# Weight conversion: the clamp on VectorE, the addition of the low words on GpSimd

## The chip, the cores and the metric

The kernel runs on one core of a Trainium2 chip. The time is the device time of one execution in microseconds (us); three executions of the kernel before took 1046.4, 1047.48 and 1050.78 us, and their median, 1047.48 us, is the time before. Engines are called by their names in the profile: PE is TensorE, DVE is VectorE, ACT is ScalarE, POOL is GpSimd, SP is SyncE, which here issues DMAs.

## The reference

Attention with mixing of heads on both sides of the softmax, and then a gated feed-forward block on its output. Cut to what is computed:

```python
scores = scale * np.matmul(q, k.transpose(0, 1, 3, 2))        # 4 batches, 12 heads, 448 x 448, head size 64
scores = np.einsum('bhij,hg->bgij', scores, w_pre)
attn   = softmax(scores)                                       # over the last axis
attn   = np.einsum('bhij,hg->bgij', attn, w_post)
x      = np.matmul(attn, v) -> 1792 tokens x 768
g      = x @ w_gate                                            # 768 x 1536
val    = x @ w_val                                             # 768 x 1536
out    = (silu(g) * val) @ w_out                               # 1536 x 768
```

The three feed-forward weights arrive as 64-bit floats (two 32-bit words each) and are made into 32-bit floats on the chip. This conversion is what the change touches.

## The kernel before

**Stages.** The attention of the four batches comes first, to about 510 us of the span. Then the tokens pass through the feed-forward block in two halves of 896 (`b` = 0 and 1). In each half the up part goes through 12 column blocks `f` of 128: per block four PE chains of 18 matmuls of 448 columns, two for the gate weight (`upg`, token halves 0 and 1) and two for the value weight (`upv`). One chain takes the high part of the weights (`whi`, L507), the low part (`wlo`, L508), and the high part with the low part of x (L512). ACT takes the silu of `upg` (`sg`, L517); DVE multiplies it with `upv` (`m`, L523), ACT rounds the product (`gh`, L528) and DVE takes the rest (`gl`, L534). The down part (`dn`, L546 to L548) follows.

**Units.** The weights are cut into 36 units of 128 x 768 numbers: units 0, 2, ... 22 are the gate weight of a block, 1, 3, ... 23 its value weight, 24 to 35 parts of `w_out`. So a block of the up part uses a pair of units, and a unit of `w_out` serves 63 matmuls. In the first half of the tokens each unit is loaded in its 64-bit form (`raw`) and converted by `convert` in nine steps; then it is stored to DRAM (`keep`) for the second half, which only loads it again. `split_w` makes `whi` on ACT (L492) and `wlo` on DVE (L488).

**The steps of `convert`.** Step 0 and 1 (ACT): absolute value (`mag`) and sign (`sgn`) of the word that holds the upper half. Step 2: clamp of `mag` from below and above (L460), one input, two operations. Steps 3 to 5 (DVE): bit shifts that make of `mag` the 32-bit float without its last bits, and in `w` its exponent (L462, L464, L466). Step 6 (DVE): the low word times the exponent (L468). Step 7 (DVE): `w = mag + w` (L470). Step 8: `w` times the sign (L472). Steps 2 and 8 are on `eng`: DVE for the units 0 to 2, which are converted beside the last batch's attention, POOL for the other 33. The tile `mag` has two buffers, `sgn` two, `w` three, `raw` two.

**Order.** Each piece of work is put on a list by `at(key, ...)` or `at_ff(key, ...)` with a number as its due time, and the list is worked off in the order of the numbers. So the numbers alone set in which order each engine gets its instructions; an engine then takes them one behind the other, and waits at each for what that one needs. `at_ff` counts the feed-forward block in matmul groups: a chain of the up part is 3.4 of them. For a unit that is due at `n`, a step with the number x is issued at `n - x`, the rounding to `whi` at `n - 3.8`, `wlo` at `n - 2.8`, the store at `n - 3.9`. All loads and stores of the weights go through SP's queue, in the order of the list.

Of the kernel before, what the change touches and what calls it, by code (L numbers as in the profile page):

```python
# [15 lines left out]
ALU = mybir.AluOpType  # L16
# [3 lines left out]
def f32_of(bits):  # L20
    return struct.unpack("<f", struct.pack("<I", bits))[0]
# [3 lines left out]
def talking_heads_moe_kernel(ctx, tc, q, k, v, w_pre, w_post, w_gate, w_val, w_out, out):  # L25
    nc = tc.nc
# [46 lines left out]
    def at(key, fn):  # L73
        ops.append((key, len(ops), fn))
# [7 lines left out]
    def later(fn, *a):  # L82
        return lambda: fn(*a)
# [267 lines left out]
    for b in range(B):  # L351
# [8 lines left out]
        for c in range(NC):  # L360

            n = n0 + first(c)
            if (b, c) == (0, 0):
                load, ready, step = -61, -31, 1.0
                score = -29.0
            else:
                before = tiles((c - 1) % NC)
                step = before / NPAIR
# [60 lines left out]
    def unit_index(u):  # L429
        if u[0] == "o":  # L430
            return 2 * NFC + u[1] * (NFC * ET // W) + u[2]
        return 2 * u[1] + (u[0] == "v")
# [9 lines left out]
    def convert(u, step):  # L442
        n = unit_index(u)
        eng = nc.vector if n < EARLY else nc.gpsimd
        if step == 0:
            mag, sgn, w = (
                pl["cv_p"].tile([P, W], F32, tag=x, name=f"{x}_{n}", bufs=k) for x, k in (("mag", 2), ("sgn", 2), ("w", 3))
            )
            cvs[u] = mag, sgn
            w32[0, u] = w  # L450
        mag, sgn = cvs[u]
        w = w32[0, u]
        low, high = raws[u][:, :, 0], raws[u].bitcast(F32)[:, :, 1]
        a, b = mag.bitcast(U32), w.bitcast(U32)
        if step == 0:
            nc.scalar.activation(mag, high, AF.Abs)  # L456
        elif step == 1:
            nc.scalar.activation(sgn, high, AF.Sign)
        elif step == 2:
            eng.tensor_scalar(mag, mag, f32_of(0x38000000), f32_of(0x47EFFFFF), op0=ALU.max, op1=ALU.min)  # L460
        elif step == 3:
            nc.vector.tensor_scalar(a, a, 0x08000000, 4, op0=ALU.bitwise_xor, op1=ALU.logical_shift_left)  # L462
        elif step == 4:
            nc.vector.tensor_scalar(b, a, 1, 0x7F800000, op0=ALU.logical_shift_right, op1=ALU.bitwise_and)  # L464
        elif step == 5:
            nc.vector.tensor_scalar(a, a, 1, None, op0=ALU.logical_shift_right)  # L466
        elif step == 6:
            nc.vector.scalar_tensor_tensor(w, low, 2.0 ** -52, w, op0=ALU.mult, op1=ALU.mult)  # L468
        elif step == 7:
            nc.vector.tensor_tensor(w, mag, w, op=ALU.add)  # L470
        else:
            eng.tensor_tensor(w, w, sgn, op=ALU.mult)  # L472

# [96 lines left out]
    def at_ff(n, fn):  # L570
        at(END + n / 1.8, fn)

    for b in range(NT // TB):
        n0 = b * span
        for i, (c, x) in enumerate((c, x) for c in range(NKC) for x in range(2)):
            if b:
                at_ff(n0 - 60 + 4.2 * i, later(load_x, b, x, c))
            else:
                at(B * NTB + (-2.8 + 0.9 * c if x else -9.6 + 1.2 * c), later(load_x, b, x, c))
        units = []  # L580
        for f in range(NFC):
            n = n0 + f * T_F
            units += [(n, ("g", f)), (n + 2 * T_H, ("v", f))]
            for hf in range(2):
                if b == f == hf == 0:
                    at(B * NTB + UPH, later(up, b, f, "g", hf, True, False))
                    at_ff(n, later(up, b, f, "g", hf, False, True))
                else:
                    at_ff(n + hf * T_H, later(up, b, f, "g", hf))
                at_ff(n + (2 + hf) * T_H, later(up, b, f, "v", hf))  # L590
                at_ff(n + (1 + hf) * T_H + 0.3, later(gate, b, f, hf))
                at_ff(n + (3 + hf) * T_H + 0.3, later(gated, b, f, hf))
                at_ff(n + (3 + hf) * T_H + 1.1, later(gated_low, b, f, hf))
        for e in range(3):
            n1 = n0 + NFC * T_F + e * NFC * T_D
            for f in range(0, NFC, W // ET):
                last = b == NT // TB - 1 and e == 2
                units.append((n1 + f * (0.6 if last else T_D), ("o", e, f // (W // ET))))
            if last:
                for c in range(NTC):  # L600
                    n = n1 + c * NFC * T_D / NTC
                    for f in range(NFC):
                        at_ff(n, later(down, b, e, f, c))
                    if c % 2 or c == NTC - 1:
                        at_ff(n + NFC * T_D / NTC + 0.1, later(finish, b, e, c - c % 2))
            else:
                for f in range(NFC):
                    for c in range(NTC):
                        at_ff(n1 + f * T_D, later(down, b, e, f, c))
                for c in range(0, NTC, 2):  # L610
                    at_ff(n1 + (NFC - 1 + (c + 2) / NTC) * T_D + 0.1, later(finish, b, e, c))
        for n, u in units:
            if b:
                at_ff(n - 16, later(load_w, b, u))
                at_ff(n - 8, later(split_w, b, u, False))
                at_ff(n - 7, later(split_w, b, u, True))
            elif unit_index(u) < EARLY:
                n = START + SPACE * unit_index(u)
                at(max(START, n - 4.0), later(load_raw, u))
                for step, x in enumerate((0.4, 0.8, 0.5, 0.5, 1.8, 2.5, 2.9, 4.1, 5.1)):  # L620
                    at(n + x + 0.25, later(convert, u, step))
                at(n + 8.4, later(split_w, b, u, False))
                at(n + 10.6, later(split_w, b, u, True))
                at(n + 6.7, later(keep, u))
            else:
                n -= LEAD
                n1 = END + (n - 21.3) / 1.8
                at(min(n1, B * NTB + 2.75) if unit_index(u) == EARLY else n1, later(load_raw, u))
                for step, x in enumerate((16.2, 15, 15.4, 12.6, 12.1, 11.6, 11.1, 10.2, 5.8)):
                    at_ff(n - x, later(convert, u, step))  # L630
                at_ff(n - 3.8, later(split_w, b, u, False))
                at_ff(n - 2.8, later(split_w, b, u, True))
                at_ff(n - 3.9, later(keep, u))
# [43 lines left out]
```

## Time and profile before

| | |
|---|---|
| time, median of three | 1047.48 us |
| the profiled execution | 1048.95 us, its span 1047.2 us |
| busy in the span | PE 97%, DVE 57%, ACT 49%, POOL 42% |
| last work of the attention on PE | at 510.6 us of the span |
| up part, first half of the tokens | to 686.7 us |
| down part, first half of the tokens | 686.7 to 776.3 us, then the second half |

The profile belongs to one execution. Its span is the time from the first to the last instruction; 1.75 us of the execution lie outside of it. A share of busy time is an average over all stages; what a change in one stage is worth is read from that stage. In the rows below, a row of a timeline has the start in us from the span's start, the duration in us, engine, line, operation, output<-inputs with their shapes, the number of instructions merged into the row, and in brackets how long the engine had been idle and what released it.

### The profile page before, as it was taken

To read this page: it belongs to the slowest core of one execution; us is meant where nothing else is said; L and a number is where in the kernel's file an instruction comes from. 1 tells how busy PE (TensorE), PEld (TensorE's weight loads), DVE (VectorE), ACT (ScalarE), POOL (GpSimd) and SP (SyncE) were. 2 spreads that over 40 slices of the span, in tenths; PEclk is the share of its full clock that TensorE was granted. 3 is DMA by queue.
4 is the path that set the end of the run, shared out by engine and by line. 5 is a ranking of instruction groups with operands and counts; after the bars stand their busy time and mean duration, and the time that the engine had idled before them with its cause. 6 is when DMAs were issued, how large, how long until landed. Compare 5 with 4: busy or idle time off the path is not lost.

```text
span 1047.2 us, 17964 instructions
## 1 busy us (share of the span) xinstructions
PE 1020.7 (97%) x6660; PEld 853.2 (81%) x6660; DVE 597.8 (57%) x1181; ACT 514.1 (49%) x1103; POOL 444.0 (42%) x439
## 2 busy tenths in 40 slices
PE   6899999999999999999999999999999999999998
PEld 3577777777777777777898888899999999999998
DVE  4566555657466565577499999998923322332110
ACT  2686776768676676786444434443322222222110
POOL 1675555647465555674375666667600000000000
PEclk9999999999999999998999999999999999999999
DMA  6466443844466443668554444448741112112311
GB/s 125 117 160 172 116 126 112 202 132 125 124 160 176 116 127 113 183 199 244 183 166 151 147 169 138 160 155 289 254 167 46 60 47 61 46 61 62 97 50 36
DMA packets 131055, 140.69 MB, mean 134 GB/s; under 512 B 52552, under 2 KB 114012, under 8 KB 130968
## 3 DMA queue, kind: packets, MB, share of 16 engines
q1 hardware_dynamic: 130776, 139.30, 45.3%
q8 instruction: 53, 0.87, 0.4%
q0 software_dynamic: 192, 0.24, 0.1%
q14 instruction: 34, 0.28, 0.1%
HBM read 70.19 MB, written 30.80 MB: 96 GB/s over the span
## 4 chain that ended last, share of the span: by engine, by line
PE 76%; DVE 13%; ACT 3%; issue 3%; DMA 3%; POOL 2%; SPq 0%; POOLq 0%; ACTq 0%; DVEq 0%
PE post L306 14%; PE qk L224 8%; PE av L328 7%; PE dn L547 5%; PE dn L546 5%; PE dn L548 5%; PE pre L271 5%; PE pre L273 3%; PE pre L272 3%; DVE w L470 3%; DVE mag L462 3%; PE upv L508 3%; PE upv L507 3%; PE upg L512 3%; PE upg L508 3%; PE upg L507 3%
## 5 line engine op out<-in xcount | busy, mean ns | idle before, releaser
L265 POOL TENSOR_TENSOR lo<-rs,hi 120x448 fp32r<-120x448 f32 x180 | 206.5, 1148 | 161.0 <-ACT hi L259 157.6
L306 PEld LDWEIGHTS post<-rw,e 120*112 120x112 f32 (+1 forms) x1440 | 169.9, 177 | 32.2 <-issue 9.6
L306 PE MATMUL post<-rw,e 120*112 120x120 f32 (+1 forms) x1440 | 181.7, 270 | 0.3 <-POOL rw L296 0.3
L460 POOL TENSOR_SCALAR mag<-mag 128x768 f32<-128x768 f32 x33 | 103.8, 3145 | 95.9 <-ACT mag L456 94.1
L547 PE MATMUL dn<-wlo,gh 128*128 128x256 f32 x504 | 141.1, 280 | 0.5 <-DVE wlo L488 0.5
L546 PE MATMUL dn<-whi,gh 128*128 128x256 f32 x504 | 141.0, 280 | 0.0
L548 PE MATMUL dn<-whi,gl 128*128 128x256 f32 x504 | 141.0, 280 | 0.0
L280 DVE TENSOR_REDUCE st<-pre 120x1 f32<-120x448 f32 x180 | 111.8, 621 | 39.8 <-PE pre L273 36.9
L315 ACT ACTIVATE attnT<-post 112x480 f32<-112x480 f32 (+3 forms) x192 | 103.5, 546 | 28.4 <-PE post L306 26.3
L287 ACT ACTIVATE e<-pre,st 120x448 f32<-120x448 f32 x180 | 114.0, 633 | 0.5 <-DVE st L280 0.5
L259 ACT ACTIVATE hi<-rs 120x448 fp32r<-120x448 f32 x180 | 103.9, 577 | 17.7 <-DMA rs<-stg 9.6
L508 PE MATMUL upv<-x,wlo 128*128 128x448 f32 x288 | 106.5, 370 | 4.7 <-DVE wlo L488 4.7
L488 DVE TENSOR_TENSOR wlo<-w,whi 128x768 fp32r<-128x768 f32 x72 | 69.1, 961 | 72.2 <-ACT whi L492 70.8
L230 DVE COPY stg<-qk 110x448 f32<-110x448 f32 (+1 forms) x144 | 85.1, 619 | 43.1 <-PE qk L224 42.5
L507 PE MATMUL upg<-x,whi 128*128 128x448 f32 x288 | 105.8, 367 | 0.0
L508 PE MATMUL upg<-x,wlo 128*128 128x448 f32 x288 | 105.6, 367 | 0.0
L507 PE MATMUL upv<-x,whi 128*128 128x448 f32 x288 | 105.6, 367 | 0.0
L224 PE MATMUL qk<-kk,qt 64*110 64x448 f32 (+1 forms) x384 | 100.3, 594 | 4.4 <-DVE stg L230 2.8
L492 ACT ACTIVATE whi<-w 128x768 fp32r<-128x768 f32 x72 | 60.2, 839 | 87.8 <-POOL w L472 57.9
L528 ACT ACTIVATE gh<-m 128x448 fp32r<-128x448 f32 x48 | 27.8, 579 | 137.8 <-DVE m L523 137.8
L547 PEld LDWEIGHTS dn<-wlo,gh 128*128 128x128 f32 x504 | 94.7, 188 | 0.7 <-DVE wlo L488 0.7
L546 PEld LDWEIGHTS dn<-whi,gh 128*128 128x128 f32 x504 | 94.7, 188 | 0.0
(65 smaller groups left out, 1786.7 us busy)
## 6 DMA issues: line engine op xcount, KB each, us to landing
rs<-stg SPq DMA_DIRECT2D x176, 210.0 KB
w_d<-w SPq DMA_DIRECT2D x36, 384.0 KB
w<-w_d SPq DMA_DIRECT2D x36, 384.0 KB
x<-x_d SPq DMA_DIRECT2D x24, 448.0 KB
x_d<-xs SPq DMA_DIRECT2D x42, 224.0 KB
raw<-in_moe_w_gate_dram SPq DMA_DIRECT2D x12, 768.0 KB
raw<-in_moe_w_val_dram SPq DMA_DIRECT2D x12, 768.0 KB
raw<-in_moe_w_out_dram SPq DMA_DIRECT2D x12, 768.0 KB
```

Of the source, the lines that this page charges most:

```text
L224: nc.tensor.matmul(pt[:m], qt[b, c][hs, p, :m], kk[b, p][hs], start=True, stop=True)
L259: nc.scalar.activation(hi[:n], x[:n], AF.Copy)
L265: nc.gpsimd.tensor_tensor(lo[:n], x[:n], hi[:n].bitcast(F32), op=ALU.subtract)
L280: nc.vector.tensor_reduce(st[:n, 0:1], pt[:n], axis=AX.X, op=ALU.max, negate=True)
L287: nc.scalar.activation(e[:n], pt[:n], AF.Exp, bias=st[:n, 0:1], scale=1.0, accum_out=st[:n, 1:2])
L306: nc.tensor.matmul(pt[:, c, :, :m], e[:n, c * CP:(c + 1) * CP], w[:n, :, :m], start=True, stop=True)
L460: eng.tensor_scalar(mag, mag, f32_of(0x38000000), f32_of(0x47EFFFFF), op0=ALU.max, op1=ALU.min)
L507: nc.tensor.matmul(pt, hi[:, c], xh[:, c, ts], start=(c == 0), stop=False)
L508: nc.tensor.matmul(pt, lo[:, c], xh[:, c, ts], start=False, stop=False)
L546: nc.tensor.matmul(pt, gh, hi, start=opens, stop=False)
L547: nc.tensor.matmul(pt, gh, lo, start=False, stop=False)
L548: nc.tensor.matmul(pt, gl, hi, start=False, stop=closes)
```

## The change

Two of the nine steps of `convert` change their engine for the units 3 to 35. The clamp (L460) goes from POOL to DVE, where it is issued together with the first bit shift; the addition (L470, now L469) goes from DVE to POOL. The units 0 to 2 keep both on DVE. The nine steps become eight, and the due numbers of the steps are set anew: the multiplication with the sign is now due at `n - 9.2` and no longer at `n - 5.8`. Lines behind the change have one number less than before (L488 becomes L487).

```diff
--- before.py
+++ after.py
@@ -457,17 +457,16 @@
         elif step == 1:
             nc.scalar.activation(sgn, high, AF.Sign)
         elif step == 2:
-            eng.tensor_scalar(mag, mag, f32_of(0x38000000), f32_of(0x47EFFFFF), op0=ALU.max, op1=ALU.min)
+            nc.vector.tensor_scalar(mag, mag, f32_of(0x38000000), f32_of(0x47EFFFFF), op0=ALU.max, op1=ALU.min)
+            nc.vector.tensor_scalar(a, a, 0x08000000, 4, op0=ALU.bitwise_xor, op1=ALU.logical_shift_left)
         elif step == 3:
-            nc.vector.tensor_scalar(a, a, 0x08000000, 4, op0=ALU.bitwise_xor, op1=ALU.logical_shift_left)
+            nc.vector.tensor_scalar(b, a, 1, 0x7F800000, op0=ALU.logical_shift_right, op1=ALU.bitwise_and)
         elif step == 4:
-            nc.vector.tensor_scalar(b, a, 1, 0x7F800000, op0=ALU.logical_shift_right, op1=ALU.bitwise_and)
+            nc.vector.tensor_scalar(a, a, 1, None, op0=ALU.logical_shift_right)
         elif step == 5:
-            nc.vector.tensor_scalar(a, a, 1, None, op0=ALU.logical_shift_right)
+            nc.vector.scalar_tensor_tensor(w, low, 2.0 ** -52, w, op0=ALU.mult, op1=ALU.mult)
         elif step == 6:
-            nc.vector.scalar_tensor_tensor(w, low, 2.0 ** -52, w, op0=ALU.mult, op1=ALU.mult)
-        elif step == 7:
-            nc.vector.tensor_tensor(w, mag, w, op=ALU.add)
+            eng.tensor_tensor(w, mag, w, op=ALU.add)
         else:
             eng.tensor_tensor(w, w, sgn, op=ALU.mult)
 
@@ -617,7 +616,7 @@
             elif unit_index(u) < EARLY:
                 n = START + SPACE * unit_index(u)
                 at(max(START, n - 4.0), later(load_raw, u))
-                for step, x in enumerate((0.4, 0.8, 0.5, 0.5, 1.8, 2.5, 2.9, 4.1, 5.1)):
+                for step, x in enumerate((0.4, 0.8, 0.7, 1.6, 2.3, 2.9, 4.1, 5.1)):
                     at(n + x + 0.25, later(convert, u, step))
                 at(n + 8.4, later(split_w, b, u, False))
                 at(n + 10.6, later(split_w, b, u, True))
@@ -626,7 +625,7 @@
                 n -= LEAD
                 n1 = END + (n - 21.3) / 1.8
                 at(min(n1, B * NTB + 2.75) if unit_index(u) == EARLY else n1, later(load_raw, u))
-                for step, x in enumerate((16.2, 15, 15.4, 12.6, 12.1, 11.6, 11.1, 10.2, 5.8)):
+                for step, x in enumerate((14.6, 14.2, 14.0, 13.4, 12.8, 12.2, 11.2, 9.2)):
                     at_ff(n - x, later(convert, u, step))
                 at_ff(n - 3.8, later(split_w, b, u, False))
                 at_ff(n - 2.8, later(split_w, b, u, True))
```

In the up part this is what stands on DVE for block 5 (its products `m_5_0` and `m_5_1`) and for the units 13 and 14, before (unit 13 is `mag_7045` and `w_7047`):

```order
L523 TENSOR_TENSOR m_5_0_7068<-sg_5_0_7007,upv_5_0_7013 128x448
L534 TENSOR_TENSOR gl_5_7071<-m_5_0_7068,gh_5_7070 128x448
L462 TENSOR_SCALAR mag_7045<-mag_7045 128x768
L523 TENSOR_TENSOR m_5_1_7099<-sg_5_1_7034,upv_5_1_7049 128x448
L464 TENSOR_SCALAR w_7047<-mag_7045 128x768
L534 TENSOR_TENSOR gl_5_7071<-m_5_1_7099,gh_5_7070 128x448
L466 TENSOR_SCALAR mag_7045<-mag_7045 128x768
L468 SCALAR_TENSOR_TENSOR w_7047<-raw_7011,w_7047 128x768
L470 TENSOR_TENSOR w_7047<-mag_7045,w_7047 128x768
L488 TENSOR_TENSOR wlo_13_7108<-w_6986,whi_13_7107 128x768
L462 TENSOR_SCALAR mag_7112<-mag_7112 128x768
L464 TENSOR_SCALAR w_7114<-mag_7112 128x768
```

and after (unit 13 is `mag_7071` and `w_7073`, unit 14 begins at `mag_7134`):

```order
L522 TENSOR_TENSOR m_5_0_7065<-sg_5_0_7004,upv_5_0_7017 128x448
L533 TENSOR_TENSOR gl_5_7068<-m_5_0_7065,gh_5_7067 128x448
L460 TENSOR_SCALAR mag_7071<-mag_7071 128x768
L461 TENSOR_SCALAR mag_7071<-mag_7071 128x768
L463 TENSOR_SCALAR w_7073<-mag_7071 128x768
L465 TENSOR_SCALAR mag_7071<-mag_7071 128x768
L522 TENSOR_TENSOR m_5_1_7101<-sg_5_1_7036,upv_5_1_7045 128x448
L467 SCALAR_TENSOR_TENSOR w_7073<-raw_7010,w_7073 128x768
L533 TENSOR_TENSOR gl_5_7068<-m_5_1_7101,gh_5_7067 128x448
L487 TENSOR_TENSOR wlo_13_7109<-w_7008,whi_13_7108 128x768
L460 TENSOR_SCALAR mag_7134<-mag_7134 128x768
L461 TENSOR_SCALAR mag_7134<-mag_7134 128x768
```

The clamp stands ahead of the first shift of each unit, the addition is gone, and the second product `m_5_1` and its rest now stand around the multiplication of the low words (L467), behind the three shifts and no longer between them. `wlo` of a unit stands, as before, behind the last DVE step of the next unit.

On POOL there stood in the same place, two operations to a unit, the clamp of one unit and the sign of the unit ahead of it (`w_6986` is unit 12, `w_7047` 13):

```order
L460 TENSOR_SCALAR mag_7045<-mag_7045 128x768
L472 TENSOR_TENSOR w_6986<-w_6986,sgn_6985 128x768
L460 TENSOR_SCALAR mag_7112<-mag_7112 128x768
L472 TENSOR_TENSOR w_7047<-w_7047,sgn_7046 128x768
L460 TENSOR_SCALAR mag_7173<-mag_7173 128x768
L472 TENSOR_TENSOR w_7114<-w_7114,sgn_7113 128x768
```

and now, again two to a unit, both of the same one (`w_7008` is unit 12, `w_7073` 13, `w_7136` 14):

```order
L469 TENSOR_TENSOR w_7008<-mag_7006,w_7008 128x768
L471 TENSOR_TENSOR w_7008<-w_7008,sgn_7007 128x768
L469 TENSOR_TENSOR w_7073<-mag_7071,w_7073 128x768
L471 TENSOR_TENSOR w_7073<-w_7073,sgn_7072 128x768
L469 TENSOR_TENSOR w_7136<-mag_7134,w_7136 128x768
L471 TENSOR_TENSOR w_7136<-w_7136,sgn_7135 128x768
```

At the end of the attention, DVE had before, with the first three operations of unit 3 (`mag_6350`) ahead of the fourth of the last attention outputs (`xs_3_3`):

```order
L340 TENSOR_TENSOR xs_3_1_6269<-av_3_1_6260,xs_3_1_6269 128x112
L340 TENSOR_TENSOR xs_3_2_6282<-av_3_2_6273,xs_3_2_6282 128x112
L462 TENSOR_SCALAR mag_6350<-mag_6350 128x768
L464 TENSOR_SCALAR w_6352<-mag_6350 128x768
L466 TENSOR_SCALAR mag_6350<-mag_6350 128x768
L340 TENSOR_TENSOR xs_3_3_6295<-av_3_3_6286,xs_3_3_6295 128x112
L468 SCALAR_TENSOR_TENSOR w_6352<-raw_6243,w_6352 128x768
```

and now:

```order
L340 TENSOR_TENSOR xs_3_1_6269<-av_3_1_6260,xs_3_1_6269 128x112
L340 TENSOR_TENSOR xs_3_2_6282<-av_3_2_6273,xs_3_2_6282 128x112
L340 TENSOR_TENSOR xs_3_3_6295<-av_3_3_6286,xs_3_3_6295 128x112
L460 TENSOR_SCALAR mag_6371<-mag_6371 128x768
L461 TENSOR_SCALAR mag_6371<-mag_6371 128x768
L463 TENSOR_SCALAR w_6373<-mag_6371 128x768
L465 TENSOR_SCALAR mag_6371<-mag_6371 128x768
L467 SCALAR_TENSOR_TENSOR w_6373<-raw_6243,w_6373 128x768
```

The fourth of these outputs stands ahead of unit 3 now. On ACT the absolute value of unit 3 has moved behind it in the same way.

## Rows read from the trace of the kernel before

**Rows 1.** The page's first part: busy us of each engine, share of the span, instructions.

```profile
PE 1020.7 (97%) x6660; PEld 853.2 (81%) x6660; DVE 597.8 (57%) x1181; ACT 514.1 (49%) x1103; POOL 444.0 (42%) x439
```

**Rows 2.** The timeline of PE in the middle of the up part: the last six matmuls of each chain, and the matmul that had to wait.

```profile
580.80 1.38 PE L512 MATMUL upg<-x,whi 128*128 128x448 f32 x6
...
584.45 1.38 PE L512 MATMUL upg<-x,whi 128*128 128x448 f32 x6
...
586.65 0.47 PE L508 MATMUL upv<-x,wlo 128*128 128x448 f32 x1 [0.62 <-DVE wlo L488]
...
588.99 1.18 PE L512 MATMUL upv<-x,whi 128*128 128x448 f32 x5
```

**Rows 3.** The same view at the second and at the last of the twelve blocks.

```profile
521.52 1.38 PE L512 MATMUL upg<-x,whi 128*128 128x448 f32 x6
...
673.62 1.38 PE L512 MATMUL upg<-x,whi 128*128 128x448 f32 x6
```

**Rows 4.** The timeline of DVE over one pair of units, from the first shift of a unit to the same shift two units on.

```profile
586.90 2.20 DVE L462 TENSOR_SCALAR mag<-mag 128x768 uint32<-128x768 uint32 x1 [0.30 <-POOL mag L460]
589.13 0.56 DVE L464 TENSOR_SCALAR w<-mag 128x768 uint32<-128x768 uint32 x1
589.73 0.56 DVE L466 TENSOR_SCALAR mag<-mag 128x768 uint32<-128x768 uint32 x1
590.20 0.95 DVE L468 SCALAR_TENSOR_TENSOR w<-raw,w 128x768 f32<-128x768 uint32 x1
591.19 1.46 DVE L470 TENSOR_TENSOR w<-mag,w 128x768 f32<-128x768 f32 x1
592.57 0.94 DVE L488 TENSOR_TENSOR wlo<-w,whi 128x768 fp32r<-128x768 f32 x1
593.44 0.61 DVE L523 TENSOR_TENSOR m<-sg,upv 128x448 f32<-128x448 f32 x1
594.70 1.40 DVE L534 TENSOR_TENSOR gl<-m,gh 128x448 fp32r<-128x448 f32 x1 [0.65 <-ACT gh L528]
596.01 0.55 DVE L462 TENSOR_SCALAR mag<-mag 128x768 uint32<-128x768 uint32 x1
596.48 0.61 DVE L523 TENSOR_TENSOR m<-sg,upv 128x448 f32<-128x448 f32 x1
597.01 0.55 DVE L464 TENSOR_SCALAR w<-mag 128x768 uint32<-128x768 uint32 x1
597.74 0.62 DVE L534 TENSOR_TENSOR gl<-m,gh 128x448 fp32r<-128x448 f32 x1 [0.18 <-ACT gh L528]
598.28 0.55 DVE L466 TENSOR_SCALAR mag<-mag 128x768 uint32<-128x768 uint32 x1
598.75 0.95 DVE L468 SCALAR_TENSOR_TENSOR w<-raw,w 128x768 f32<-128x768 uint32 x1
599.73 1.46 DVE L470 TENSOR_TENSOR w<-mag,w 128x768 f32<-128x768 f32 x1
...
602.36 2.20 DVE L462 TENSOR_SCALAR mag<-mag 128x768 uint32<-128x768 uint32 x1 [0.30 <-POOL mag L460]
```

**Rows 5.** The timeline of POOL over the same stretch.

```profile
583.88 2.98 POOL L460 TENSOR_SCALAR mag<-mag 128x768 f32<-128x768 f32 x1 [3.74 <-ACT mag L456]
586.83 1.85 POOL L472 TENSOR_TENSOR w<-w,sgn 128x768 f32<-128x768 f32 x1
590.45 3.33 POOL L460 TENSOR_SCALAR mag<-mag 128x768 f32<-128x768 f32 x1 [1.77 <-ACT mag L456]
593.76 1.85 POOL L472 TENSOR_TENSOR w<-w,sgn 128x768 f32<-128x768 f32 x1
```

**Rows 6.** Two rows of the timelines of POOL and DVE in the attention, where a subtraction on POOL and a `wlo` meet.

```profile
475.69 1.13 POOL L265 TENSOR_TENSOR lo<-rs,hi 120x448 fp32r<-120x448 f32 x1 [0.55 <-ACT hi L259]
476.04 1.60 DVE L488 TENSOR_TENSOR wlo<-w,whi 128x768 fp32r<-128x768 f32 x1
```

**Rows 7.** The instructions of the lines of the clamp and of the sign: duration in ns (least, median, most), first and last start.

```profile
L460 POOL TENSOR_SCALAR mag<-mag x33: 2776/3183/3346, 505.8 to 749.5; 128x768 f32<-128x768 f32 x33
L460 DVE TENSOR_SCALAR mag<-mag x3: 548/555/690, 450.7 to 474.4; 128x768 f32<-128x768 f32 x3
L472 POOL TENSOR_TENSOR w<-w,sgn x33: 1837/1848/2438, 516.1 to 759.3; 128x768 f32<-128x768 f32 x33
```

**Rows 8.** The timelines at the end of the attention: one row of PE, and three of DVE.

```profile
510.56 0.99 PE L328 MATMUL av<-attnT,vn 112*64 112x112 f32 x16 [1.39 <-DVE xs L340]
508.58 0.56 DVE L462 TENSOR_SCALAR mag<-mag 128x768 uint32<-128x768 uint32 x1 [2.44 <-POOL mag L460]
510.24 0.27 DVE L340 TENSOR_TENSOR xs<-av,xs 128x112 fp32r<-128x112 f32 x1
511.41 0.96 DVE L470 TENSOR_TENSOR w<-mag,w 128x768 f32<-128x768 f32 x1
```

**Rows 9.** Busy us of the engines in three stretches: length, PE, its weight loads, DVE, ACT, POOL, then the granted clock of PE as a share of full speed, share and GB/s of the DMA engines.

```profile
471.00:474.38 3.38, 1.69 (x12) 1.43 (x12) 3.35 (x6) 3.38 (x10) 3.38 (x4) 0.95 0.93 272
474.40:478.00 3.60, 3.60 (x21) 2.71 (x22) 3.53 (x8) 2.08 (x5) 1.88 (x3) 0.50 0.95 270
...
686.66:776.30 89.64, 89.14 (x758) 88.94 (x757) 68.29 (x72) 30.66 (x40) 50.49 (x20) 1.00 0.65 220
```

**Rows 10.** The waits of PE behind the first half's up part: who waited for whom, us in total, times, longest.

```profile
PE dn L547 <- DVE wlo L488: 0.5, 1, 0.5
```

## The prediction

> **What bounds the kernel now.** The page's first part is read first: PE is busy 97% of the span, every other engine under 60% [rows 1]. So a change off PE can only alter the little time in which PE waits, and the question is where it waits for the conversion. The waits of PE and then its timeline show that. In the up part of the first half a chain of 18 matmuls takes 3.65 us, start to start (580.80 to 584.45), but the first value chain of each block takes 4.54 (584.45 to 588.99), since its second matmul waits for `wlo` from DVE [rows 2]. Unhindered a block takes 4 x 3.65 = 14.60. From block 1 to block 11 the trace has 673.62 - 521.52 = 152.10 us for ten blocks, 6.10 more than 146.0 [rows 3]; with the 0.89 of the last block the conversion costs PE 7.0 us here. That is all that a faster conversion can win in this part.
>
> Next is the timeline of DVE over one pair of units, which is one block [rows 4]. From 586.90 to 602.36 it is 15.46 us, and DVE is hardly idle: 0.30 + 0.65 + 0.18 = 1.13. So a pair of units takes as long as DVE needs, and PE is held to that. But several rows are longer than the same instruction elsewhere: L462 takes 2.20 and 0.55, L534 1.40 and 0.62, L470 1.46 both times against 0.96 where POOL stands still [rows 4, 8]. The surplus is 1.65 + 0.78 + 2 x 0.50 = 3.43, and it falls together with POOL's operations [rows 5]. What is left, 15.46 - 1.13 - 3.43 = 10.90, is DVE's own work.
>
> **How the two engines exclude each other.** The multiplication L472 starts at 586.83 and takes 1.85; L462, issued at 586.90, ends at 589.10 and needs 0.55, so it was let in at 588.55, 1.72 behind POOL's start and 0.13 before its end. The next L472 starts at 593.76; L534, issued at 594.70, ends at 596.10 and needs 0.62, so again it got in at 595.48, 1.72 behind [rows 4, 5]. A subtraction on POOL, also with two inputs, let a `wlo` in 1.00 behind its start, again 0.13 before its end [rows 6]. So a POOL operation on two tiles keeps such DVE operations out nearly for its whole length. The clamp does not. The one at 590.45 is held up first: L468 runs to 591.15, and the clamp takes 3.33 instead of its least 2.78 [rows 4, 5, 7]; then L470, issued at 591.19, waits only to 591.69. So the clamp keeps DVE out for 0.54, and who asks first goes first. The product `m`, which reads PSUM, takes 0.61 beside POOL and without it [rows 4].
>
> **Term 1: the pair of units.** On DVE's own work: an addition goes; L468 to L488 takes 592.57 - 590.20 = 2.37, less the wait of 0.50 is 1.87, and 0.87 remains without the addition (L488 to the next row), so 2 x 1.00 is saved. A clamp comes, 0.55 by the three that DVE has done [rows 7], with the gap to the shift behind it 0.59, so 2 x 0.59 is added. The second `m` and `gl` now stand elsewhere; their neighbours overlap less or more by some 0.08 each, together +0.07. Own work: 10.90 - 2.00 + 1.18 + 0.07 = 10.15. Idle: the 0.65 for `gh` stays, the 0.30 for POOL's clamp goes, some 0.1 for `whi` stays: 0.75.
>
> The waits decide. The trace has no addition of these tiles on POOL. Its bounds are the shortest hold and the longest in the rows, 0.54 (the clamp) and 1.72 (L472); I take 1.72, since L472 has the same shape and two inputs and the subtraction behaved alike; less than 0.54 is excluded, as two tiles must be read. So POOL holds 4 x 1.72 = 6.88 per pair, against 2 x (1.72 + 0.54) = 4.52. Laid along the new order: (a) behind L467 of the pair's second unit comes `wlo`, issued before the addition; the addition waits for it and runs beside `m` and the idle time for `gh`; `gl` meets its last 0.37. (b) The multiplication follows behind `gl`; the clamp of the next unit, issued 0.08 before `gl` ends, waits for all of it, 1.64. (c) Behind that unit's L467 `gl` is first, then the addition, then `wlo`, which waits 1.56: it cannot come earlier, because its `whi` stands on ACT behind a `gh` that waits for `m`. (d) The multiplication follows on `wlo`, and the next clamp waits 1.64. Sum 5.21. A pair takes 10.15 + 0.75 + 5.21 = 16.1 us: DVE works less and waits more. PE then waits 1.5 in each block.
>
> Block 3 is the first to feel it (1.05), eight follow: 1.05 + 8 x 1.50 = 13.05. Against 7.0 this is **+6.05**. POOL, with 4 x 1.85 per pair, stays far from full; ACT's waits for the sign go, but nothing hung on them.
>
> The Trainium skill says otherwise of the clamp: by "SBUF — State Buffer", section "Who interferes with whom", a GpSimd operation and a VectorE operation of these kinds exclude each other for the whole instruction, whoever issues first. For the multiplication the trace agrees (1.72 of 1.85); for the clamp it does not, as L470 waited 0.50 at one that had over two us to run and `wlo` ran beside it in 0.94. By that rule the clamp would be the long hold, 2.78, and its removal a gain; this is the first rival's case.
>
> **Term 2: the end of the attention.** PE stood 1.39 because an output copy on DVE (510.24) was queued behind unit 3's L462, which waited 2.44 for POOL's clamp [rows 8]. This copy now stands ahead of unit 3: **-1.4**. Unit 3 itself is needed a block later. Bounds -1.4 and 0.
>
> **Term 3: the down part.** Per unit DVE's own work is 4 x 0.55 + 2 x 0.87, about 4.0 with gaps, and at most 2 x 1.64 of waits, 7.3; PE takes 89.64 / 12 = 7.47 for a unit [rows 9]. That fits, barely. Only the hand-over from the up part, 0.5 before [rows 10], grows with the backlog by about 0.65 per pair: **+0.7**, bounds 0 and 2.
>
> **The rest.** In the units 0 to 2 two operations of 0.55 trade places with a reduction of the softmax; behind it ACT waits for PE, so nothing, bounds -1.1 and +1.1. SP's queue has the same sequence; stores come earlier, loads wait for L467 as for L468 before: nothing, with PE busy in front of them as cover.
>
> Sum: 6.05 - 1.4 + 0.7 = +5.4, on the profiled execution 1048.95 to 1054.3. That one lies 1.5 above the median; on the median of 1047.48 I forecast **1052.9**.
>
> **Rivals.** *Faster: POOL's addition holds DVE briefly.* If it holds like the clamp, (a) and (c) nearly vanish, and a pair needs 14.3 or less, under PE's 14.60. PE then no longer waits: -7.0 - 1.4 - 0.5 = 1038.6. The page's rule gives the same time, since holds of 2 x (2.78 + 1.85) would fall to 4 x 1.85, 1.9 less than now, and 15.46 - 1.9 is below 14.60 too. For it: POOL's busy time falls, the clamp's hold is short. Against it: both two-input operations in the rows. 0.13.
>
> *No change: a POOL operation falls into DVE's idle time.* If `gl` waits longer for `gh`, the multiplication of (b) goes ahead of it and half of its hold lies in the idle time; a pair takes about 15.4, and the total is 9 x (15.4 - 15.46) - 1.4 + 0.7, some 1046.3. For it: 0.65 of idle time stands right there; against it: the addition ends 0.37 after `gl` is issued, so `gl` is ahead. 0.20.
>
> *Slower still: DVE falls behind in the down part and PE's clock gives way.* It decides when a unit costs DVE more than 7.47: 0.3 more than my 7.3 is 0.13 per unit over 12 units, 1.6. And where PE had worked 1.69 of 3.38 us its granted clock stood at half for the next stretch, 0.50 [rows 9]; one such fall over some 7 us costs 3.4. 1052.9 + 1.6 + 3.4 = 1057.9. Against it: in the up part PE would still work nine tenths of the time. 0.11.
>
> **How the numbers follow.** The forecast has 0.56, with a range of its own from 1049.5 to 1056.5: each 0.06 in a hold is worth some 1.4 us in the total. A measurement tells 0.5%, 5.2 us, from no change; the line lies at 1052.7, so of the 0.56 I count 0.35 as slower and 0.21 as the same. With the rivals: slower 0.46, same 0.41, faster 0.13. The range for 8 in 10 leaves out most of the fast rival and the end of the slow one: 1041 to 1059.
>
> **What would show it.** Right: blocks 3 to 11 take 16.1; `wlo` (L487) takes 2.5 every other time, the clamp on DVE 2.2, the shifts 0.55; the first value chain of a block waits some 1.4; POOL's addition takes 1.85 or a little more, and the 1.39 at 510 is gone. Wrong: blocks of 14.6 with no wait of PE, `wlo` at 0.95 beside POOL's addition, or POOL's addition far from 1.85.

## The result and the profile after

Five executions of the changed kernel took 1051.71 to 1055.61 us, median 1054.39; five of the kernel before took 1046.4 to 1050.78 us, median 1047.48. The medians lie 6.9 us apart; the ratio over all ten executions is 1.0056, 95% interval 1.0038 to 1.0073. By the ratio the change makes the kernel some 5.9 us slower. 1052.9 us, slower, was the forecast.

The shares of the page's first part hardly differ from [rows 1]:

```profile
PE 1018.7 (97%) x6660; PEld 854.4 (81%) x6660; DVE 613.7 (58%) x1181; ACT 512.4 (49%) x1103; POOL 429.9 (41%) x439
```

DVE's busy time has risen by 16 us although it has 33 additions fewer and 33 clamps more, and a clamp is the shorter instruction. So busy time here holds waiting. The waits of PE, and the weight loads of the same line in the page's groups (busy us, mean ns | idle us before them and what ended it):

```profile
PE upv L507 <- DVE wlo L487: 11.4, 9, 1.4
...
PE dn L546 <- DVE wlo L487: 1.3, 1, 1.3
```

```profile
L507 PEld LDWEIGHTS upv<-x,wlo 128*128 128x128 f32 x288 | 54.1, 188 | 19.0 <-DVE wlo L487 14.8
```

The nine waits are the nine blocks from 3 to 11. A matmul that starts late is preceded by a weight load that started late, and that row gives the whole delay: 14.8, some 1.6 per block. The timeline of PE over one block shows the same:

```profile
617.52 1.38 PE L511 MATMUL upg<-x,whi 128*128 128x448 f32 x6
620.44 0.47 PE L507 MATMUL upv<-x,wlo 128*128 128x448 f32 x1 [1.34 <-DVE wlo L487]
622.77 1.38 PE L511 MATMUL upv<-x,whi 128*128 128x448 f32 x6
626.42 1.38 PE L511 MATMUL upv<-x,whi 128*128 128x448 f32 x6
```

The first value chain of the block takes 622.77 - 617.52 = 5.25, where it took 4.54 before [rows 2]; the next takes 3.65 as ever.

The stages: the first row of the value chains, of the down part and of the second half, after,

```profile
510.31 0.36 PE L506 MATMUL upv<-x,whi 128*128 128x448 f32 x1
...
692.43 0.28 PE L545 MATMUL dn<-whi,gh 128*128 128x256 f32 x1
...
783.66 0.37 PE L506 MATMUL upg<-x,whi 128*128 128x448 f32 x1
```

and before (its down part begins at 686.66, [rows 9]):

```profile
511.79 0.36 PE L507 MATMUL upv<-x,whi 128*128 128x448 f32 x1
...
776.21 0.37 PE L507 MATMUL upg<-x,whi 128*128 128x448 f32 x1
```

| stage, us | before | after | difference |
|---|---|---|---|
| to the first value chain | 511.79 | 510.31 | -1.48 |
| up part, first half | 174.87 | 182.12 | +7.25 |
| down part, first half | 89.55 | 91.23 | +1.68 |
| second half to the end of the span | 271.0 | 267.5 | -3.5 |
| span | 1047.2 | 1051.2 | +4.0 |

The first three rows are taken as the change, +7.45 (some 0.8 of the third is no wait for the conversion, as the account of term 3 shows). The last is not: the second half converts nothing, and the last section shows what differs there.

DVE over one pair of units, from the rest `gl` to the same one a block later:

```profile
611.00 1.02 DVE L533 TENSOR_TENSOR gl<-m,gh 128x448 fp32r<-128x448 f32 x1 [0.65 <-ACT gh L527]
611.94 2.20 DVE L460 TENSOR_SCALAR mag<-mag 128x768 f32<-128x768 f32 x1
614.18 0.56 DVE L461 TENSOR_SCALAR mag<-mag 128x768 uint32<-128x768 uint32 x1
...
617.25 0.62 DVE L533 TENSOR_TENSOR gl<-m,gh 128x448 fp32r<-128x448 f32 x1
617.84 2.55 DVE L487 TENSOR_TENSOR wlo<-w,whi 128x768 fp32r<-128x768 f32 x1
620.31 2.19 DVE L460 TENSOR_SCALAR mag<-mag 128x768 f32<-128x768 f32 x1
...
625.07 0.95 DVE L487 TENSOR_TENSOR wlo<-w,whi 128x768 fp32r<-128x768 f32 x1
625.94 0.61 DVE L522 TENSOR_TENSOR m<-sg,upv 128x448 f32<-128x448 f32 x1
627.20 1.02 DVE L533 TENSOR_TENSOR gl<-m,gh 128x448 fp32r<-128x448 f32 x1 [0.65 <-ACT gh L527]
```

and POOL beside it:

```profile
609.03 2.50 POOL L469 TENSOR_TENSOR w<-mag,w 128x768 f32<-128x768 f32 x1 [3.15 <-DVE w L467]
611.62 2.12 POOL L471 TENSOR_TENSOR w<-w,sgn 128x768 f32<-128x768 f32 x1
617.41 2.16 POOL L469 TENSOR_TENSOR w<-mag,w 128x768 f32<-128x768 f32 x1 [3.68 <-DVE w L467]
619.65 2.43 POOL L471 TENSOR_TENSOR w<-w,sgn 128x768 f32<-128x768 f32 x1
```

The pair takes 627.20 - 611.00 = 16.20, where it took 15.46 [rows 4]. Four rows are too long, by 1.02 - 0.62 = 0.40, 2.20 - 0.55 = 1.65, 2.55 - 0.95 = 1.60 and 2.19 - 0.55 = 1.64; together 5.29, against 3.43 before. Each of these waits ends 0.13 to 0.15 before the end of one of POOL's four operations: the first clamp, for example, needs 0.55, ends at 614.14 and so was let in at 613.59, and POOL's multiplication ends at 613.74. The second `wlo`, which finds POOL idle, takes 0.95, and the product `m`, which reads PSUM, takes 0.61 while POOL's addition runs.

### The profile page after: what moved, and what is told of

It is laid out like the page before. It is cut to its first block, busy times and chain, and to the rows that moved or that the text cites. A ratio compares the mean times of both kernels' runs of the same rounds, so it can differ in the third digit from the quotient of the medians.

```text
span 1051.2 us, 17985 instructions
## 1 busy us (share of the span) xinstructions
PE 1018.7 (97%) x6660; PEld 854.4 (81%) x6660; DVE 613.7 (58%) x1181; ACT 512.4 (49%) x1103; POOL 429.9 (41%) x439
## 4 chain that ended last, share of the span: by engine, by line
PE 77%; DVE 18%; DMA 2%; ACT 2%; issue 1%; SPq 0%; POOL 0%; ACTq 0%; DVEq 0%
PE post L306 14%; PE qk L224 8%; PE av L328 7%; PE dn L546 5%; PE dn L545 5%; PE dn L547 5%; PE pre L271 5%; DVE mag L460 5%; DVE wlo L487 4%; PE pre L273 3%; PE pre L272 3%; PE upg L511 3%; PE upg L506 3%; PE upg L507 3%; PE upv L511 3%; PE upv L506 3%
## 5 line engine op out<-in xcount | busy, mean ns | idle before, releaser
L487 DVE TENSOR_TENSOR wlo<-w,whi 128x768 fp32r<-128x768 f32 x72 | 88.7, 1234 | 73.3 <-ACT whi L491 71.8
L469 POOL TENSOR_TENSOR w<-mag,w 128x768 f32<-128x768 f32 x33 | 77.8, 2358 | 121.8 <-DVE w L467 119.2
L507 PE MATMUL upv<-x,wlo 128*128 128x448 f32 x288 | 106.2, 369 | 11.4 <-DVE wlo L487 11.4
```

The costliest lines, as they stand in the source:

```text
L487: nc.vector.tensor_tensor(lo, w, hi.bitcast(F32), op=ALU.subtract)
L507: nc.tensor.matmul(pt, lo[:, c], xh[:, c, ts], start=False, stop=False)
```

## The experiments

The theory: POOL's operation on two tiles keeps DVE's instructions on such tiles out for nearly its whole length, so that a pair is as long as DVE's work and POOL's holds together. The rivals: the due numbers did it; the clamp is slow at its new place; the longer chain of hand-overs between the engines did it; POOL is simply too slow. What the eight runs gave, all but one in one table (PE's wait is that of matmuls for `wlo` in the up part; the up part unhindered is 46 chains of 3.65, 167.9; in the run with half of the addition its chains take 3.72 throughout, which makes 171.1 without any wait, and the last section shows this second pace). Where one execution was taken, its time is marked so; such a time can be off by some us, so the up part and the pair weigh more there:

| kernel | POOL's operations for a unit | time, us | up part | PE's wait | pair on DVE |
|---|---|---|---|---|---|
| before | clamp, sign | 1047.48 | 174.87 | 4.7 | 15.46 |
| after | addition, sign | 1054.39 | 182.12 | 11.4 | 16.20 |
| due numbers of before | addition, sign | 1051.04 (one) | 179.54 | 9.1 | 16.08 |
| 3/4 of the addition | addition, sign | 1046.34 (one) | 173.97 | 3.5 | 15.40 |
| half of the addition | addition, sign | 1037.71 (one) | 171.12 | 0 | 14.88 |
| one input in place of the sign | addition, clamp form | 1038.17 (one) | 171.72 | 1.1 | 15.15 |
| sign on DVE | clamp | 1039.44 | 167.93 | 0 | 14.65 |
| addition on DVE | sign | 1036.33 | 167.80 | 0 | 14.75 |
| all on DVE | none | 1033.25 | 167.80 | 0 | 14.71 |

**The addition back on DVE**, the clamp left there:

```diff
-            eng.tensor_tensor(w, mag, w, op=ALU.add)
+            nc.vector.tensor_tensor(w, mag, w, op=ALU.add)
```

> The changed kernel with the addition back on DVE: clamp and addition on DVE, only the sign on POOL, due numbers as changed. Theory: one two-input operation a unit is left on POOL; behind wlo it falls beside m and the idle time before gl in one unit and costs some 0.4, in the other some 1.4; DVE's own work 10.15 + 2.0, idle 0.7, waits 1.8, about 14.6 or less: a block of 14.60, no wait of PE for wlo, total about 1047.5 - 7.0 - 1.4 - 0.5 = 1038.6. Rival (DVE's load): 16.2 + 1.9 = 18.1 us a pair, slower than the changed kernel by some 17 us. Rival (the clamp itself takes 2.2 us on DVE at this place): the clamp stays at 2.2 in both units.

Measured: 1036.33 us, ratio to before 0.9907 (0.9881 to 0.9934). PE's list of waits has no row for `wlo`. DVE, and POOL's only operation:

```profile
611.51 2.21 DVE L460 TENSOR_SCALAR mag<-mag 128x768 f32<-128x768 f32 x1
...
616.40 0.96 DVE L469 TENSOR_TENSOR w<-mag,w 128x768 f32<-128x768 f32 x1
...
620.34 0.55 DVE L460 TENSOR_SCALAR mag<-mag 128x768 f32<-128x768 f32 x1
```

```profile
610.95 2.34 POOL L471 TENSOR_TENSOR w<-w,sgn 128x768 f32<-128x768 f32 x1 [5.77 <-DVE w L469]
617.59 2.35 POOL L471 TENSOR_TENSOR w<-w,sgn 128x768 f32<-128x768 f32 x1 [4.30 <-DVE w L469]
```

The same clamp takes 2.21 behind POOL's sign and 0.55 in the other unit of the pair, where POOL is idle: it is not slow at its place. DVE has two instructions more than after the change, and the pair is 1.45 shorter. The time is 2.3 us below the expected 1038.6.

**The other half alone**: the kernel before, with the sign on DVE and the clamp left on POOL.

```diff
-            eng.tensor_tensor(w, w, sgn, op=ALU.mult)
+            nc.vector.tensor_tensor(w, w, sgn, op=ALU.mult)
...
-                for step, x in enumerate((16.2, 15, 15.4, 12.6, 12.1, 11.6, 11.1, 10.2, 5.8)):
+                for step, x in enumerate((16.2, 15, 15.4, 12.6, 12.1, 11.6, 11.1, 10.2, 9.8)):
```

> The kernel before, with the sign (L472) on DVE as well, so that POOL keeps only the clamp. Theory (DVE and POOL exclude each other; a two-input operation on POOL costs DVE some 1.7 us, the clamp 0.54): DVE gets two operations of 0.95 more in each pair of units and loses the waits of 1.65 and 0.78; own work 10.90 + 2 x 0.88, idle 0.7, waits 2 x 0.5, about 14.2 to 14.6 us, so a block is at PE's 14.60 and PE waits little or not at all for wlo. Total about 1047.5 - 7.0 - 0.5 = 1040, with the 1.39 at the end of the attention still there. Rival (DVE's load is what counts, as it is the engine that is never idle): 15.46 + 1.9 = 17.2 us a pair, the total some 15 us slower than before.

Measured: 1039.44 us, ratio 0.9934 (0.9910 to 0.9958). The rows of DVE that meet POOL's clamp, which here starts at 610.51 and 616.94:

```profile
610.92 1.46 DVE L470 TENSOR_TENSOR w<-mag,w 128x768 f32<-128x768 f32 x1
...
617.86 1.39 DVE L472 TENSOR_TENSOR w<-w,sgn 128x768 f32<-128x768 f32 x1
```

Each waits 0.5 or less at a POOL operation of 3 us. The up part is 6.94 shorter than before, so already the kernel before lost its 7 us there to the multiplication on POOL.

**One input in place of two**: after the change, POOL's multiplication replaced by the clamp's form on one tile.

```diff
-            eng.tensor_tensor(w, w, sgn, op=ALU.mult)
+            if n < EARLY:
+                nc.vector.tensor_tensor(w, w, sgn, op=ALU.mult)
+            else:
+                nc.gpsimd.tensor_scalar(w, w, f32_of(0x38000000), f32_of(0x47EFFFFF), op0=ALU.max, op1=ALU.min)
```

> The changed kernel, but for the units 3 to 35 the sign on POOL is left out and in its place w is clamped there, an operation on one input that takes 2.78 us where the sign took 1.84. The sign is not applied, so the output is another. Theory (the hold counts, not POOL's time): the hold falls from 1.72 to 0.54, the clamp on DVE from 2.20 to 0.55 to 1.1, a block to 14.6. Rival (the way through POOL is too long for wlo): POOL's way for a unit is 0.9 longer, a block stays at 16.2 or grows. Rival (the clamp on DVE is a slow operation): it stays at 2.2.

Measured: 1038.17 us. POOL's operation (now L474), and DVE beside it:

```profile
610.98 3.69 POOL L474 TENSOR_SCALAR w<-w 128x768 f32<-128x768 f32 x1
...
618.62 3.36 POOL L474 TENSOR_SCALAR w<-w 128x768 f32<-128x768 f32 x1
```

```profile
618.94 1.18 DVE L460 TENSOR_SCALAR mag<-mag 128x768 f32<-128x768 f32 x1
620.15 0.56 DVE L461 TENSOR_SCALAR mag<-mag 128x768 uint32<-128x768 uint32 x1
...
621.34 1.06 DVE L465 TENSOR_SCALAR mag<-mag 128x768 uint32<-128x768 uint32 x1
```

POOL works over an us longer per unit than with the sign, with as many hand-overs, and the up part is 10.4 us shorter than after the change. POOL's own length and the chain of hand-overs are therefore not what costs; what POOL keeps out of DVE is. The pair of 15.15 is longer than the expected 14.6: in each unit a shift (621.34) waits as well as the clamp, so this form holds DVE twice and not once.

**The old due numbers** with the new engines:

```diff
-                for step, x in enumerate((14.6, 14.2, 14.0, 13.4, 12.8, 12.2, 11.2, 9.2)):
+                for step, x in enumerate((16.2, 15, 12.6, 12.1, 11.6, 11.1, 10.2, 5.8)):
```

> The changed kernel's engines with due numbers like those of before (16.2, 15, 12.6 for clamp and first shift, 12.1, 11.6, 11.1, 10.2, 5.8). Theory: POOL holds as long as in the changed kernel, four times 1.72 in a pair, and a block takes 15.8 to 16.3. Rival (the new due numbers did it): a block of 15.5 or less, like before.

Measured: 1051.04 us, a pair of 627.15 - 611.07 = 16.08. In the second unit of the pair the shift is now held as well as the clamp:

```profile
612.01 2.20 DVE L460 TENSOR_SCALAR mag<-mag 128x768 f32<-128x768 f32 x1
...
618.73 2.20 DVE L460 TENSOR_SCALAR mag<-mag 128x768 f32<-128x768 f32 x1
620.97 2.08 DVE L461 TENSOR_SCALAR mag<-mag 128x768 uint32<-128x768 uint32 x1
```

Another order only moves the holds to other rows: `wlo` has 0.95 in this kernel, and a shift 2.08. The due numbers are at most 0.12 of the pair. They are more of the up part, 2.58 of its +7.25: with the old ones PE waits in eight blocks and not in nine. This rests on one execution; the other 4.67 come with the engines alone.

**A part of the addition.** Only the first 576 of 768 columns:

```diff
-            eng.tensor_tensor(w, mag, w, op=ALU.add)
+            m = W if n < EARLY else W * 3 // 4
+            eng.tensor_tensor(w[:, :m], mag[:, :m], w[:, :m], op=ALU.add)
```

> The changed kernel with POOL's addition on the first 576 of the 768 columns of each unit; the low words of the other 192 columns are not added. Order, number of instructions and what waits for what stay the same. Theory (POOL's two-input operations keep DVE out nearly for their whole length): a quarter less of the addition is some 0.5 less hold. In the pair of 16.20 the wait of gl (0.40) goes and the wait of wlo (1.60) shrinks to some 1.1; the clamps still wait 1.64 each. A pair takes 16.20 - 0.40 - 0.50 = 15.3, PE waits about 0.7 in each block, and the one time is 9 x 0.9, about 8, below the changed kernel's: some 1046. Rival A (the hand-over itself costs: the addition is one more step between two engines, whatever its length): a pair stays at 16.2, 1054. Rival B (DVE is simply slow at the new place of the clamp): a pair stays at 16.2 too, as the clamps are untouched.

Measured: 1046.34 us; POOL and DVE:

```profile
612.48 1.75 POOL L470 TENSOR_TENSOR w<-mag,w 128x576 f32<-128x576 f32 x1 [3.69 <-DVE w L467]
```

```profile
599.57 2.20 DVE L460 TENSOR_SCALAR mag<-mag 128x768 f32<-128x768 f32 x1
...
612.92 2.13 DVE L488 TENSOR_TENSOR wlo<-w,whi 128x768 fp32r<-128x768 f32 x1
614.97 2.19 DVE L460 TENSOR_SCALAR mag<-mag 128x768 f32<-128x768 f32 x1
```

The addition is 2.16 - 1.75 = 0.41 shorter, and the `wlo` behind it waits 2.13 - 0.95 = 1.18 instead of 1.60: 0.42 less. The pair is 15.40, and the up part 8.15 shorter than after the change, as the theory had it. That the whole time also comes out at the expected 1046 is in part luck: the second half is 3.4 longer than after the change, for the reason in the last section.

**Half of it** (`W // 2` in the same line). In a first execution PE's granted clock was 0.58 in the mean of the whole span and the time was 1589.43 us, from which nothing follows for the change:

> As the run with three quarters, with POOL's addition on the first 384 columns of each unit; the low words of the other 384 are not added. Theory: half of the addition is some 1.0 less hold than with all of it; gl's 0.40 goes, wlo's 1.60 shrinks to 0.6: a pair would be 16.20 - 0.40 - 1.00 = 14.8, and PE, whose block is 14.60 unhindered, waits for wlo 0.2 per block or less. The one time is 9 x 1.4, some 12.6, below the changed kernel's: about 1041. If the cost fell with the length in proportion down to nothing it would go on falling towards the 1036 of the kernel with the addition on DVE. Rivals A (the hand-over costs) and B (the clamp's place costs): 16.2 and 1054 again.

Two of its rows can still be read, one of DVE and one of POOL:

```profile
969.04 1.71 DVE L488 TENSOR_TENSOR wlo<-w,whi 128x768 fp32r<-128x768 f32 x1
```

```profile
977.83 1.01 POOL L470 TENSOR_TENSOR w<-mag,w 128x384 f32<-128x384 f32 x1 [5.40 <-DVE w L467]
```

`wlo` waits 0.76 although PE's clock is so much lower, and half of the addition takes 1.01 where DVE is idle. The kernel was run once more:

> The kernel with half of POOL's addition (384 of 768 columns; the low words of the other 384 are not added) once more, because in its first execution PE's granted clock stood at 0.58 over the whole span. The run with three quarters fell by 0.8 us per pair, from 16.20 to 15.40, of which 0.42 is the shorter hold at wlo. Theory: the next quarter takes another 0.4 off wlo's wait (1.18 to some 0.75) and the addition no longer meets anything else, so a pair takes 15.40 - 0.4 = 15.0 or a little less, PE waits some 0.4 in each block, and the one time is 9 x 0.4, about 4, below the 1046.3 with three quarters: some 1042. If only the length of the addition counted, and not what it meets, it would be 0.8 per pair again: 14.6 and 1039. The rivals that speak of the hand-over or of the clamp's place have 15.40 again, 1046.

Measured: 1037.71 us, below what the theory gave (1042).

```profile
616.26 1.85 POOL L472 TENSOR_TENSOR w<-w,sgn 128x768 f32<-128x768 f32 x1
```

```profile
616.50 0.62 DVE L523 TENSOR_TENSOR m<-sg,upv 128x448 f32<-128x448 f32 x1 [1.19 <-PE upv L512]
617.77 0.83 DVE L534 TENSOR_TENSOR gl<-m,gh 128x448 fp32r<-128x448 f32 x1 [0.65 <-ACT gh L528]
...
622.82 1.72 DVE L488 TENSOR_TENSOR wlo<-w,whi 128x768 fp32r<-128x768 f32 x1
```

`wlo` waits 0.77, again 0.41 less, as expected. The pair is 14.88, 0.52 less and not 0.4, and PE waits for no `wlo` where 0.4 a block was expected. For now DVE waits for PE (1.19 ahead of `m`), and POOL's multiplication at 616.26 lies in DVE's idle time and beside `m` and keeps out only `gl`, for 0.21. Once DVE is no longer the bound, part of the holds costs nothing; the expectation had carried them on unchanged. The miss in the whole time, 4.3, comes from elsewhere for the most part: of the 8.6 between the two runs 3.5 lie in the second half, which converts nothing.

**All on DVE**: clamp, addition and sign.

```diff
-            eng.tensor_tensor(w, mag, w, op=ALU.add)
+            nc.vector.tensor_tensor(w, mag, w, op=ALU.add)
...
-            eng.tensor_tensor(w, w, sgn, op=ALU.mult)
+            nc.vector.tensor_tensor(w, w, sgn, op=ALU.mult)
```

> The changed kernel with clamp, addition and sign all on DVE; POOL has nothing in the conversion. Theory: DVE's own work grows by 2 x 1.0 for the additions and 2 x 1.0 for the signs, 10.15 + 4.0 = 14.15, the idle time of 0.75 stays, the waits of 5.29 go: a pair takes 14.6 (PE's pace) to 14.9, and PE waits at most 0.3 in a block. 1036 to 1040, so beside the two kernels that keep one operation on POOL (1036.3 and 1039.4), and 14 to 18 below the changed kernel, although DVE does four operations of a pair more. Rival (DVE is full, and POOL is needed for the conversion): DVE's work of before, 10.90 + 3.43 + 1.13 = 15.46, plus 2 x 0.59 for clamps and 2 x 1.0 for signs, is 18.6 a pair, 9 x 2.4 = 22 above the changed kernel: 1076.

Measured: 1033.25 us, ratio 0.9868 (0.9832 to 0.9903).

```profile
604.05 0.56 DVE L460 TENSOR_SCALAR mag<-mag 128x768 f32<-128x768 f32 x1 [0.17 <-ACT mag L456]
...
609.12 0.95 DVE L487 TENSOR_TENSOR wlo<-w,whi 128x768 fp32r<-128x768 f32 x1
609.99 0.95 DVE L471 TENSOR_TENSOR w<-w,sgn 128x768 f32<-128x768 f32 x1
...
618.76 0.56 DVE L460 TENSOR_SCALAR mag<-mag 128x768 f32<-128x768 f32 x1 [0.17 <-ACT mag L456]
```

No row is longer than its least, and a pair takes 618.76 - 604.05 = 14.71, as expected, with four instructions more on DVE than after the change. The time lies below the expected 1036 to 1040, and below both kernels, before and after. Against the addition alone on DVE it was not timed side by side; the intervals overlap, and up part (167.80) and down part (88.70) are the same in both, so which of the two is better stays open.

## Why the prediction was right, step by step

**Term 1, the pair of units.** Forecast 16.1 with waits of 0.37, 1.64, 1.56 and 1.64 at `gl`, clamp, `wlo`, clamp; measured 16.20 with 0.40, 1.65, 1.60 and 1.64, at these instructions in this order. The choice that carried it was the upper bound, 1.72, for an operation that the trace did not show; the runs with a part of the addition show that a hold does go with the length. The sum was too small: +6.05 against +7.25. A stalled block cost 1.60 and not 1.50, which is 0.8 over eight blocks; the first one, block 3, cost 1.45 and not 1.05. The prediction did not ask what the new due numbers are worth by themselves; the run with the old ones has +4.67 in this part.

POOL's addition takes 2.16 and 2.50, not "1.85 or a little more". POOL waits too: it is issued at 617.41 while `gl` (617.25, 0.62) still runs. With 0.31 of waiting in 2.16, its own length is 1.85, and each quarter of the columns is 0.41 of it; half of it, 1.03 by this, took 1.01 in the run at the low clock, where POOL did not wait.

By the Trainium skill, "SBUF — State Buffer", section "Who interferes with whom", the exclusion is a lock: the instruction that is issued first has it for its whole length, and the other one blocks. For operations on two tiles the runs agree to 0.13 to 0.15 before the end: 1.60, 1.18, 0.77 of wait at `wlo` for 4/4, 3/4 and 2/4 of the addition. For the form with one input they do not: beside POOL's 3.36 us at 618.62 a shift ran at 620.15 in 0.56.

**Term 2, the end of the attention.** Forecast -1.4, measured -1.48; the row of 1.39 ahead of `av` [rows 8] is gone, and that shows the term. That the sizes agree so well is luck: among the runs in which this wait is gone the first value chain starts anywhere from 507.83 to 510.89. In the run with the sign on DVE, which keeps the old order there, PE still waits 1.7 for the output copy. The text ahead of the prediction says that the due numbers alone set the order. That is too short: `xs_3_3` has a smaller due number than unit 3 and still stood behind its shifts, so the order depends on something else too; what that is stays open.

**Term 3, the down part.** Forecast +0.7, bounds 0 and 2; measured +1.68, of which the hand-over is 1.3 - 0.5 = 0.8. The rest is no wait for the conversion: behind the hand-over PE waits for no `wlo`, but the 63 matmuls of a unit mostly take 7.48 after and 7.39 before.

**The rest** was put at nothing. Sum +5.4 forecast, +7.45 by stages in the one pair of profiles, +5.9 (4.0 to 7.6) by the ratio. The direction, the instructions that wait and the length of the holds were right by their mechanism; that the sum comes within 0.5 of the ratio is in part luck, since by stages the up part was put 1.2 too low.

**The rivals.** *POOL's addition holds briefly* fell: it holds for nearly as long as it lasts. Its price was sound, since kernels in which PE does not wait take 1033 to 1039, and it gave 1038.6. *A POOL operation falls into DVE's idle time* did not happen after the change, where the addition held `gl` for 0.40 and the multiplication came behind it; it did happen with half of the addition. *Slower still* did not happen: behind the hand-over no unit of the down part made PE wait, and the granted clock was 1.00 in the up part and the down part.

## What to carry to other kernels

In this kernel work that was moved from VectorE to GpSimd was not taken off VectorE, since both worked on 32-bit tiles in SBUF and the GpSimd operation read two of them. So ask how long the GpSimd operation keeps VectorE out, and add that to VectorE's chain; here an addition of 0.95 on VectorE became a hold of up to 1.60 there. Read it from rows of one instruction that are longer beside the other engine than alone. And when an engine's busy time rises with less work on it, look for waiting inside its rows; here that was the whole surplus.

## What was not expected of the hardware

**Two paces of the same matmuls.** In the second half, with nothing to wait for and the granted clock at 1.00 in both, the chains of the profiled execution of before take 3.72 us,

```profile
808.45 1.40 PE L512 MATMUL upg<-x,whi 128*128 128x448 f32 x6
812.17 1.40 PE L512 MATMUL upg<-x,whi 128*128 128x448 f32 x6
```

and those of after 3.65:

```profile
807.98 1.38 PE L511 MATMUL upv<-x,whi 128*128 128x448 f32 x6
811.63 1.38 PE L511 MATMUL upv<-x,whi 128*128 128x448 f32 x6
```

`wlo` on DVE takes 0.96 there in both, so only PE is slower, by 1.9%. One execution can have both paces: the run with half of the addition has 3.72 in the up part and 3.65 in the second half, which takes 267.5 us; the run with three quarters has mostly 3.65 in the up part and 3.72 in the second half, which takes 271.0. The second half is the same work in all these kernels, so the difference there is not the conversion's. It is worth 3.5 us in one half and hides part of the change between the two spans. Whether it goes with the kernel or with the execution can't be told from one profile of each, and its cause was not tried.

**POOL's form with one input holds at both ends.** Beside POOL's L474, from 618.62 to 621.98, the clamp waited 0.63, until 619.57; the shift at 621.34 waited 0.50, until 0.14 before POOL's end; between them shifts ran at 0.56. So for a shift the 0.54 that the prediction took for the clamp is the first of two holds. A subtraction of two tiles was not held at the end: in the run with the sign on DVE, POOL's clamp that starts at 616.94 ends at 620.39, and beside it

```profile
619.18 0.94 DVE L488 TENSOR_TENSOR wlo<-w,whi 128x768 fp32r<-128x768 f32 x1
```

which is its least. Why the two differ was not tried. POOL's form with one input also takes longer than the multiplication of two tiles, 2.78 at least against 1.84 [rows 7].
